# RWKV-7 scan with a hardswish FFN on one Trainium2 core: the PSUM layout and the order of the FFN after the first group

## The chip, the cores and the metric

The kernel runs on one core of one Trainium2 chip. The metric is the device time of one launch in microseconds; lower is better. Before the change the median of three runs is 794.57 us (792.73 to 795.51).

## The reference

Inputs are r, k, v, w, a, b of shape (batch 4, heads 8, time 768, head size 40) and two FFN matrices of 320 x 2048 and 2048 x 320, all float32. For every batch and head a 40 x 40 state is carried over time, and then the heads are joined to 320 features per token and go through the FFN:

```python
for t in range(S):
    y[:, :, t] = einsum('bhd,bhde->bhe', rt, state)
    Sa = einsum('bhde,bhe->bhd', state, at)
    state = state * wt[:, :, None, :] - einsum('bhd,bhe->bhde', Sa, bt) + einsum('bhd,bhe->bhde', vt, kt)
x = y.transpose(0, 2, 1, 3).reshape(B * S, H * D)   # 3072 x 320
h = x @ w_in
out = (h * clip(h + 3.0, 0.0, 6.0) / 6.0) @ w_out
```

## The kernel before, in words

**Units.** Time is cut into blocks of 64 steps. A unit is one such block for two batches, so its 128 tokens fill the 128 partitions. There are 24 units (`NK`), in groups of four (`NU`): 12 blocks of time by two pairs of batches. Neighbouring units belong to different pairs of batches, so a state is handed on from unit i to unit i + 2.

**Stages.** A unit is first prepared (`prepare`) and later stepped (`step`). Each stage is a generator: up to `yield PE` it issues its TensorE work into PSUM, after it the evictions by ScalarE (ACT) or VectorE (DVE). Preparing has W (turn w, copy it to `wm`, scan it to `prods`), gam (a second scan and the decay factors), A, B, K (turn and scale), F, factor, E and EV. Stepping has RT and VT (turn r and v), R, C, S (turn the state), U, UT, rS, H, y (output and new state) and the moves that bring the output to the FFN's layout. "Turn" is a transpose on TensorE against an identity matrix. `turn_pairs` (line 474) does it with four transposes of 128 x 128 into one bank. `turn_halves` (line 484) does it with eight of 64 rows each, even and odd ones into the two banks of a pair. In this kernel r and v are turned as halves from unit 4 on, a and b from unit 8 on; w and k are always turned as pairs, and the state in the same full-height form at line 879.

**Inversion.** Each group of four units needs the inverse of a triangular matrix. It is solved by `invert`, a side stream of about 67 small steps: 30 times a product (line 746) and a sum (line 752) on DVE, with three DVE transposes. `aside(n)` puts n of these steps into the instruction order. `third_block` finishes the inverse on TensorE (lines 781 and 804) into `tinv`.

**FFN.** A unit's FFN is two jobs, r = 0 and 1, each over half of the 2048 hidden columns. `expand` (line 1079) multiplies by w_in into two one-bank tiles `h`, in four pieces of four 128 x 128 matmuls, and then `short` adds the last 64 features (16 matmuls of 64 rows in the records). `results` makes `gt` out of each bank: a ReLU on ACT (line 1094), then a minimum and a product on DVE (line 1095), which reads the bank again. `contract` (line 1120) multiplies `gt` by w_out in four pieces of two matmuls 320 wide. The order of one stream is: expand of a job, then contract of the job before it. From unit 2 on both jobs of a unit add up in the one bank `o`, and ACT writes it out once as `ob` (line 1138); for units 0 and 1 each job is evicted by itself, as `part` by ACT (line 1130) and `ob` by DVE with `part` added (line 1135).

**Order.** The order on each engine is written out by hand. After the first group the loop goes over units 4 to 23 and in each over four blocks, 80 in all, numbered m. `a_block(m)` collects the stages that are due, those of stepping and those of preparing ahead. Where a unit ahead began at a multiple of four they are one part, otherwise two, and `together` issues a part: all TensorE products first, then all evictions in the order of `RESULTS`. `feed` puts FFN pieces between, by rates of 2.8, 3.5, 4.5 or 6.2 pieces per block (times 8/9 once `spread` is set), and 2 or 3 inversion steps per piece while an inversion is on. With `spread`, `short` of an open job is called in `together`, after the turns of W, S and K.

**PSUM.** It has eight banks. After the first group's FFN has begun they are: two pairs (four banks) for the stages, the bank `one` for the turns of W, S and K, the bank `o` for the FFN's output, and two banks `h`.

Of the kernel before, what the change touches and what calls it, by code (L numbers as in the profile page):

```python
# [16 lines left out]
P = 128  # L17
BL = 64
# [13 lines left out]
def kernel(  # L32
# [62 lines left out]
    ctx.enter_context(tc.manual_schedule())  # L95

    def bank(tag, shape, bufs):
        return ps.tile(shape, F32, name=tag, tag=tag, bufs=bufs)

    ring, open_half = deque(), [None]  # L100
    lent = tc.tile_pool(name="lent", bufs=1, space=PSUM)
    pools = {"lent": lent.__enter__(), "pair": ps}
    pairs = deque([("pair", 2), ("pair", 2), ("lent", 1)])

    def pair():
# [5 lines left out]
    def begun_ffn():  # L111

        lent.__exit__(None, None, None)
        pairs.clear()
        pairs.append(("pair", 2))
        pools["h"] = ctx.enter_context(tc.tile_pool(name="hidden", bufs=1, space=PSUM))

# [20 lines left out]

    shared = [None, 0]

    def ps_pair(*dims):

        n = 1
        for d in dims:
            n *= d
        if shared[0] is None or shared[1] + n > 512:
            shared[:] = pair(), 0
            open_half[0] = None
        at = shared[1]
        shared[1] += n  # L150
        views, step = [], n
        for d in dims:
            step //= d
            views.append([step, d])
        t = shared[0][:]
        return [_ap(t, at, views), _ap(t, at + 512, views), _ap(t, at, [[512, 2]] + views)]
# [56 lines left out]
    for t in wms:  # L213
        nc.vector.memset(t[:], 0.0)
    store = const.tile([P, 2 * H * BOTH], F32, name="store")
    slots = [store[:, n * H * BL:(n + 1) * H * BL].rearrange("p (h t) -> p h t", h=H) for n in range(3)]
    by_v, by_u = (store[:, n * H * BOTH:(n + 1) * H * BOTH].rearrange("p (h t) -> p h t", h=H) for n in range(2))
    inputs, others = {}, {}
# [310 lines left out]
    def prepare(i, F):  # L529
        n, o = i % NU, data[i]  # L530
        halves = i >= 2 * NU
        def w_stage():
            wt = turn_pairs(o["WN"])
            yield PE

            wm = o["wm"] = wms[i % 2]
            wv = wm[:, 0:SCAN].rearrange("p (r m i) -> p r m i", m=2, i=HB + 1)
            x = wt[:].rearrange("p r (q m i) -> p (r q) m i", q=2, m=2)
            if i == 0:
                nc.vector.tensor_copy(wv[:, :, 0, 1:HB + 1], x[:, :, 0, ::-1])  # L540
            else:
                nc.scalar.activation(out=wv[:, :, 0, 1:HB + 1], in_=x[:, :, 0, ::-1], func=AF.Copy)
            if i == 0:
                nc.vector.tensor_copy(wv[:, :, 1, 1:HB + 1], x[:, :, 1, :])
            else:
                nc.scalar.activation(out=wv[:, :, 1, 1:HB + 1], in_=x[:, :, 1, :], func=AF.Copy)  # L546
            fetch("W", following(i))
            prods = o["prods"] = tmp.tile([P, NB, 2, HB + 1], F32, name="prods", bufs=2)
            nc.vector.tensor_tensor_scan(  # L549
                out=prods[:].rearrange("p r m i -> p (r m i)"), data0=wm[:, 0:SCAN], data1=start[:],  # L550
                initial=0.0, op0=ALU.mult, op1=ALU.add,
            )
# [124 lines left out]
        def k_stage():  # L677
            x = turn_pairs(o["KN"])
            yield PE
            kt = o["kt"] = turned("kt")  # L680
            nc.vector.tensor_tensor(out=kt[:], in0=x[:], in1=o["rg"][:], op=ALU.mult)

# [142 lines left out]
    def step(i):  # L825
# [48 lines left out]
        def s_S():  # L874

            sp = ps_any([P, 2, 2, P])
            for q in range(2):
                for j in range(2):
                    nc.tensor.transpose(out=sp[:, q, j, :],
                                        in_=st[:, q, 2 * j:2 * j + 2, :].rearrange("p r d -> p (r d)"),  # L880
                                        identity=ident[:])
            yield PE
            S = m["S"] = grp.tile([P, 2, 2, P], F32, name="S", tag="S", bufs=1)
            nc.scalar.activation(out=S[:], in_=sp[:], func=AF.Copy)

# [157 lines left out]
    sums = {}  # L1043
    narrow, spread, LATEST = [], [False], 2

# [6 lines left out]
    def feed_forward():  # L1052

        last = None
        while True:
            while not available():
                if last:
                    yield from contract(*last)
                    last = None
                yield None  # L1060
# [12 lines left out]
    def expand(xt, j0, gts):  # L1073
# [17 lines left out]
        def results():  # L1091
            for c in range(2):
                gt = ffn.tile([P, NQ, P], F32, name="gt", bufs=5)
                nc.scalar.activation(out=gt[:], in_=hp[c][:], func=AF.Relu, bias=three[:], scale=1.0)  # L1094
                nc.vector.scalar_tensor_tensor(out=gt[:], in0=gt[:], scalar=6.0, in1=hp[c][:],  # L1095
                                               op0=ALU.min, op1=ALU.mult)
                gts.append(gt)

        narrow.append(short)
        for c in range(2):  # L1100
            for t in range(2):
# [3 lines left out]
                if c == 1 and t == 1 and not narrow:  # L1105
                    results()
                yield True
        if not spread[0] and narrow:
# [3 lines left out]
    def contract(i, r, gts):  # L1112
        split = i < SPLIT
        if r == 0 or split:
            op = bank("o", [P, 512], 1)[:, 0:DM]
        else:
            op = sums.pop(i)
        for c in range(2):
            for n in range(NQ):
# [4 lines left out]
                if n % 2 and (c == 0 or n < NQ - 1):  # L1124
                    yield True
        if r == 0:
# [5 lines left out]
        else:  # L1132
# [8 lines left out]
            for q in range(2):  # L1141
                row = (2 * p + q) * T + g * BL
                queue = nc.scalar if q and i == NK - 1 else nc.sync
                queue.dma_start(out=out[row:row + BL, :], in_=ob[half(q)])
        yield True

# [88 lines left out]
    for n, x in enumerate(BESIDE):  # L1235
# [6 lines left out]
        run(chains[int(x[0])], 1, MIXED if n >= 12 else 0)  # L1242
    TURNS_IN = [("one", 1), ("pair", 2), ("pair", 2)]
    blocks = {}
# [85 lines left out]
    for _ in range(18):  # L1330
# [12 lines left out]

    PRODUCTS = ["W", "S", "K", "RT", "VT", "A", "B", "factor",
                "y", "EV", "R", "C", "U", "UT", "rS", "H", "E", "F"]
    RESULTS = ["RT", "y", "W", "VT", "EV", "R", "S", "C", "A", "B", "move", "move2",
               "U", "UT", "rS", "F", "K", "H", "E", "factor", "beside", "gam"]
    TURNS = PRODUCTS[:3]
    WIDTH = {"R": NPR * D, "U": NPR * D, "y": NPR * BOTH, "EV": NPR * D}
    BLOCKS = 4  # L1350
    FIRST_NARROW = PRODUCTS[len(TURNS)]

    def together(stages):

        begun, banks = [], 0

        def finish():
            begun.sort(key=lambda x: RESULTS.index(x[0]))
            for _, rest in begun:
                for _ in rest:  # L1360
                    pass
            begun.clear()
            shared[0] = open_half[0] = None
            ring.clear()
            ring.extend(TURNS_IN)

        for name in PRODUCTS:
            if name == FIRST_NARROW and narrow and spread[0] and stages:
                narrow[0]()
            for stage in stages.get(name, []):  # L1370
                if name in TURNS:
                    need = 2 * (open_half[0] is None) if ring[0][0] == "pair" else 1
                else:
                    width = WIDTH.get(name, NPR * BL)
                    need = 2 * (shared[0] is None or shared[1] + width > 512)
                if banks + need > 5:
                    finish()
                    banks, need = 0, 1 if name in TURNS else 2
                banks += need
                rest = stage()  # L1380
                next(rest)
                begun.append((name, rest))
        begun.extend((name, stage()) for name in stages if name not in PRODUCTS
                     for stage in stages[name])
        finish()

# [24 lines left out]

    def feed(n, inversion):

        whole = int(n)
        for k in range(whole):
            pieces(1)
            aside(inversion)
        pieces(n - whole)

    for t in (by_v, by_u):  # L1420
        nc.gpsimd.memset(t[:, :, 0:BL], 0.0)
    del score[1:]
    m = 0
    for i in range(NU, NK):
        spread[0] = i >= 2 * NU - 1
        for j in range(BLOCKS):
            rate, inversion = 3.5, 0
            if i + AHEAD >= NK + NU - 1:
                rate = 4.5
            if i < 2 * NU - 1:  # L1430
                rate = 2.8
            parts = a_block(m)
            next(parts)
            if side or i % NU == NU - 1 and rate < 4:

                rate, inversion = 6.2, 2 + (i < 2 * NU)
            feed(rate / 2, inversion)
            for _ in parts:
                pass
            if i % NU < 2 and j < 2:  # L1440
                if i % NU == 0:
                    aside(3 * L)
                block(i, j)
            if side:
                rate, inversion = 6.2, 2 + (i < 2 * NU)
            feed(rate / 2, inversion)
            m += 1
# [37 lines left out]
```

## Time and profile before

| | |
|---|---|
| median of three runs | 794.57 us |
| time of the profiled execution | 794.59 us |
| its span, first to last instruction | 792.9 us |
| TensorE (PE) busy | 727.6 us, 92% of the span |
| PE busy with the FFN, lines 1079 and 1120 | 251.2 and 230.2 us |
| DVE, ACT, POOL busy | 496.8, 307.1, 161.5 us |
| mean granted TensorE clock | 0.961 of full speed |

The span is some 1.7 us shorter than the time of its execution, and the execution is that of the median to 0.02 us, so differences in the span can be set against the median. The first 196 us are the loading of the weights, the first group and the preparing of the second; the loop that the change rewrites starts near 196.6 us, and its last product of a step is followed by FFN work alone up to the end. The slices of the page are 19.8 us each.

### The profile page before, as it was taken

The numbers are of one execution on the slowest core, as the hardware profiler recorded it, in microseconds if no ns is written. First come the engines' busy times: TensorE is split into PE (matmuls) and PEld (weight loads), VectorE is DVE, ScalarE is ACT, GpSimd is POOL, SyncE is SP. The second block draws the span as 40 slices with busy tenths as digits, with TensorE's granted clock in tenths as the row PEclk, the third lists the DMA queues.
The fourth block names the chain that finished last, engine by engine and source line by source line (L and its number), as shares of the span: only waits on it lengthen the run. The fifth ranks groups of instructions, "written<-read, shape, count | busy, mean of one in ns | idle before, by whom it ended". The sixth has DMA issues, their size and how long they took to land.

```text
span 792.9 us, 32747 instructions
## 1 busy us (share of the span) xinstructions
PE 727.6 (92%) x14552; PEld 615.8 (78%) x14552; DVE 496.8 (63%) x986; ACT 307.1 (39%) x648; POOL 161.5 (20%) x296
## 2 busy tenths in 40 slices
PE   5735778999999999999999999999999999999997
PEld 4624667878778878888888888788888888888886
DVE  7898887689446699445898345888335982323210
ACT  2347663222553424443324453334443324412211
POOL 6403012421223203112303121303111201000000
PEclk9756898999999999999999999999999999999999
DMA  9683662420334321333323233223233101110100
GB/s 121 118 201 84 156 149 51 77 49 9 65 61 76 70 55 31 65 59 62 58 42 58 49 60 70 43 46 56 51 59 58 21 19 38 38 34 13 21 19 17
DMA packets 195004, 48.14 MB, mean 61 GB/s; under 512 B 178224, under 2 KB 193584, under 8 KB 194864
## 3 DMA queue, kind: packets, MB, share of 16 engines
q1 hardware_dynamic: 190560, 45.31, 30.9%
q8 instruction: 115, 1.88, 1.0%
q10 hardware_dynamic: 4304, 0.74, 0.7%
q14 instruction: 25, 0.20, 0.1%
HBM read 34.08 MB, written 3.93 MB: 48 GB/s over the span
## 4 chain that ended last, share of the span: by engine, by line
PE 76%; DVE 10%; issue 4%; DMA 3%; SPq 2%; ACT 2%; POOL 1%; DVEq 0%; POOLq 0%; ACTq 0%
PE h L1079 26%; PE o L1120 24%; PE pair L512 4%; PE pair L975 4%; PE one L474 2%; PE pair L484 2%; PE pair L893 2%; PE pair L861 2%; PE pair L695 1%; DVE wm L560 1%; DVE prods L549 1%; PE pair L929 1%; PE pair L913 1%; DVE prod L746 1%; DVE x L752 1%
## 5 line engine op out<-in xcount | busy, mean ns | idle before, releaser
L1079 PE MATMUL h<-xt,win 128*128 128x128 f32 (+1 forms) x2304 | 251.2, 283 | 4.9 <-DVE gt L1095 4.9
L1079 PEld LDWEIGHTS h<-xt,win 128*128 128x128 f32 (+1 forms) x2304 | 231.6, 193 | 23.0 <-issue 4.4
L1120 PE MATMUL o<-wout,gt 128*128 128x320 f32 x768 | 230.2, 443 | 0.0
L1120 PEld LDWEIGHTS o<-wout,gt 128*128 128x128 f32 x768 | 138.3, 190 | 50.7
L1094 ACT ACTIVATE gt<-h,three 128x512 f32<-128x512 f32 x96 | 63.1, 687 | 110.9 <-PE h L1079 110.5
L1095 DVE SCALAR_TENSOR_TENSOR gt<-gt,h 128x512 f32<-128x512 f32 x96 | 62.2, 683 | 67.2 <-ACT gt L1094 66.9
L746 DVE TENSOR_TENSOR prod<-x 128x30 f32<-128x30 f32 (+9 forms) x180 | 65.0, 361 | 9.0 <-POOL x L731 3.5
L525 DVE COPY_PREDICATED store<-mask,pair 128x512 f32<-128x512 int32 x40 | 29.0, 725 | 62.6 <-PE pair L512 62.5
L752 DVE TENSOR_TENSOR x<-x,prod 128x30 f32<-128x30 f32 (+9 forms) x180 | 64.4, 358 | 5.5
L668 POOL TENSOR_TENSOR KBt<-K,rgt 128x320 f32<-128x320 f32 x19 | 16.4, 865 | 204.5 <-ACT rgt L657 184.4
L983 POOL TENSOR_TENSOR yg<-ys,gam 128x512 f32<-128x512 f32 x20 | 25.5, 1273 | 147.5 <-DMA R<-in_r_dram 69.6
L982 DVE TENSOR_TENSOR ys<-pair,ys 128x512 f32<-128x512 f32 x20 | 13.8, 690 | 48.7 <-PE pair L975 43.5
L549 DVE TENSOR_TENSOR_SCAN prods<-wm,start 128x528 f32<-128x528 f32 x24 | 33.5, 1401 | 10.7 <-ACT wm L546 10.2
L839 ACT ACTIVATE RT<-pair 128x512 f32<-128x512 f32 x21 | 12.5, 597 | 59.1 <-PE pair L484 59.0
L975 PE MATMUL pair<-store,KBt 64*64 64x104 f32 x1280 | 33.1, 252 | 0.0
L560 DVE TENSOR_TENSOR_SCAN wm<-wm,start 128x528 f32<-128x528 f32 x24 | 31.1, 1297 | 0.8
L700 ACT ACTIVATE EV<-pair 64x320 f32<-64x320 f32 x44 | 18.9, 430 | 31.8 <-PE pair L695 30.4
L1138 ACT ACTIVATE ob<-o 128x320 f32<-128x320 f32 x22 | 9.6, 436 | 55.3 <-PE o L1120 34.6
L975 PEld LDWEIGHTS pair<-store,KBt 64*64 64x64 f32 x1280 | 29.1, 133 | 1.5
L814 ACT ACTIVATE tinv<-pair 32x256 f32<-32x256 f32 x48 | 18.0, 375 | 31.0 <-PE pair L804 30.4
L865 DVE TENSOR_TENSOR RR<-pair,EV 128x320 f32<-128x320 f32 x21 | 10.3, 489 | 23.7 <-PE pair L512 20.5
L897 ACT ACTIVATE store<-pair 128x320 f32<-128x320 f32 x24 | 10.5, 437 | 37.0 <-PE pair L913 33.6
(278 smaller groups left out, 1072.4 us busy)
## 6 DMA issues: line engine op xcount, KB each, us to landing
V<-in_v_dram SPq DMA_DIRECT2D x96, 40.0 KB
out_dram<-ob SPq DMA_DIRECT2D x47, 80.0 KB
R<-in_r_dram SPq DMA_DIRECT2D x92, 40.0 KB
B<-in_b_dram SPq DMA_DIRECT2D x42, 80.0 KB
store<-V SPq DMA_DIRECT2D x20, 160.0 KB
W<-in_w_dram SPq DMA_DIRECT2D x37, 80.0 KB
A<-in_a_dram SPq DMA_DIRECT2D x37, 80.0 KB
K<-in_k_dram SPq DMA_DIRECT2D x37, 80.0 KB
```

The costliest lines, as they stand in the source:

```text
L512: nc.tensor.matmul(out=o[i][half(q), n, :], lhsT=lhs[half(i, D), n ^ (2 * q * swap), half(q)], rhs=rhs[half(i, D), n ^ (2 * q * back), hal ...
L525: nc.vector.copy_predicated(out=x[:, :, 0:BL].rearrange("p (h i) t -> p i h t", i=2), mask=mask8, data=o[2])
L549: nc.vector.tensor_tensor_scan(out=prods[:].rearrange("p r m i -> p (r m i)"), data0=wm[:, 0:SCAN], data1=start[:], initial=0.0, op0=ALU.m ...
L560: nc.vector.tensor_tensor_scan(out=back, data0=back, data1=start[:], initial=0.0, op0=ALU.mult, op1=ALU.add)
L746: nc.vector.tensor_tensor(out=pv, in0=_ap(x[:], (i + 1) * L + i, [[L, n], [0, i]]), in1=_ap(x[:], i * L, [[0, n], [1, i]]), op=ALU.mult,)
L752: nc.vector.tensor_tensor(out=rest, in0=rest, in1=pv, op=ALU.add)
L975: nc.tensor.matmul(out=y[q][half(s), pr, :], lhsT=o[name][half(q), h * D:h * D + SLOT], rhs=m[name][half(q), x, :], start=(name == "K" and ...
L983: nc.gpsimd.tensor_tensor(out=yg[:], in0=m["ys"][:].rearrange("p r q t -> p r (q t)"), in1=o["G"][:], op=ALU.mult)
L1079: nc.tensor.matmul(out=hp[c][:, i, :], lhsT=lhsT, rhs=rhs, start=(begun[c] == 0), stop=(begun[c] == 3 * NQ - 1))
L1094: nc.scalar.activation(out=gt[:], in_=hp[c][:], func=AF.Relu, bias=three[:], scale=1.0)
L1095: nc.vector.scalar_tensor_tensor(out=gt[:], in0=gt[:], scalar=6.0, in1=hp[c][:], op0=ALU.min, op1=ALU.mult)
L1120: nc.tensor.matmul(out=op[:], lhsT=gts[c][:, n, :], rhs=wout[:, c * HJ + r * NQ + n, :], start=((split or r == 0) and c == 0 and n == 0), ...
```

## The change

The first group, up to the loop, keeps its order but for the size of a ring of buffers (`gt`, four in place of five) and the place of three buffers in SBUF. From the loop on:

- The FFN is first led to a fixed place (`held`): the job in hand is expanded and the one before it is contracted. Then the banks `one`, `o` and the two `h` are given back. Two of them become a third pair, the other two are `h` again.
- `contract` has no bank of its own. It takes the next of the two `h` buffers, which is the bank of the first product of the job that was just expanded. So both jobs of a unit are evicted one by one: `part` by ACT for the first, `ob` by DVE for the second.
- w and k (from unit 8 on) and the state (from unit 4 on) are turned as halves, in pairs of banks.
- `together` deals a part's products to three pairs (`dealt`), mixing as few pairs as possible between those that ACT and those that DVE evicts. `short` comes ahead of all products of a block.
- Both parts of a block are issued one after the other, and the FFN pieces come after them, a number per block from the table `GAPS`. A feed also ends where a job has been expanded. `third_block` goes into the middle of a feed. Inversion steps go by the table `SHARES`: so many after each kind of piece (2, 0, 1, 0 after the four of expand, 3, 3, 3, 2 after the four of contract), one more per piece before unit 8, one within `results` and one per `together`.

```diff
-        return ps.tile(shape, F32, name=tag, tag=tag, bufs=bufs)
+        return singles.tile(shape, F32, name=tag, tag=tag, bufs=bufs)
...
         def w_stage():
-            wt = turn_pairs(o["WN"])
+            wt = turn_halves(o["WN"])[2] if halves else turn_pairs(o["WN"])
...
         def k_stage():
-            x = turn_pairs(o["KN"])
+            x = turn_in(o["KN"], halves)
...
         def s_S():
-            sp = ps_any([P, 2, 2, P])
+            sp = ps_pair(4, SLOT) if halves else ps_any([P, 2, 2, P])
...
+                    if halves:
+                        for s in range(2):
+                            nc.tensor.transpose(out=sp[s][:, 2 * q + j, :], in_=x[half(s)],
+                                                identity=ident[half(s), half(s)])
...
+    SHARES = "20103332111"
+    held, dense = [False], [False]
...
         def results():
             for c in range(2):
-                gt = ffn.tile([P, NQ, P], F32, name="gt", bufs=5)
+                gt = ffn.tile([P, NQ, P], F32, name="gt", bufs=4)
                 nc.scalar.activation(out=gt[:], in_=hp[c][:], func=AF.Relu, bias=three[:], scale=1.0)
+                if c == 0 and dense[0]:
+                    aside(int(SHARES[9]))
...
     def contract(i, r, gts):
-        split = i < SPLIT
-        if r == 0 or split:
+        split = i < SPLIT or dense[0]
+        if dense[0] and spread[0]:
+            op = pools["h"].tile([P, 512], F32, name="h", tag="h", bufs=2)[:, 0:DM]
+        elif dense[0]:
+            op = pair()[:, 0, 0:DM]
+        elif r == 0 or split:
             op = bank("o", [P, 512], 1)[:, 0:DM]
...
+        if todo and narrow and spread[0]:
+            narrow[0]()
+        while todo or others:
+            n = len(todo)
+            while dealt([x[0] for x in todo[:n]]) is None:
+                n -= 1
+            groups = dealt([x[0] for x in todo[:n]])
...
+            begun.sort(key=lambda x: RESULTS.index(x[0]))
+            aside(int(SHARES[10]))
...
+    def feed(n, more, beside=None):
+        for k in range(n):
+            if beside and k == n // 2:
+                beside()
+                beside = None
+            said = next(stream)
+            if said is None:
+                break
+            aside(int(SHARES[said - 1]) + more)
+            if said == ENDED:
+                break
...
+    held[0] = True
+    while next(stream):
+        pass
+    held[0] = False
+    ended = hidden.pop()
+    ended.__exit__(None, None, None)
+    single.__exit__(None, None, None)
+    pools["third"] = ctx.enter_context(tc.tile_pool(name="third", bufs=1, space=PSUM))
+    pools["h"] = ctx.enter_context(tc.tile_pool(name="later", bufs=1, space=PSUM))
+    pairs.append(("third", 1))
+    pairs.appendleft(("pair", 2))
+    dense[0] = spread[0] = True
...
+    GAPS = "22231244621448824244222244844844242444244484884461144244448448482142442664444423"
     for i in range(NU, NK):
-        spread[0] = i >= 2 * NU - 1
         for j in range(BLOCKS):
-            rate, inversion = 3.5, 0
...
-            parts = a_block(m)
-            next(parts)
-            if side or i % NU == NU - 1 and rate < 4:
-                rate, inversion = 6.2, 2 + (i < 2 * NU)
-            feed(rate / 2, inversion)
-            for _ in parts:
+            n = int(GAPS[m])
+            for _ in a_block(m):
                 pass
+            beside = None
             if i % NU < 2 and j < 2:
                 if i % NU == 0:
                     aside(3 * L)
-                block(i, j)
-            if side:
-                rate, inversion = 6.2, 2 + (i < 2 * NU)
-            feed(rate / 2, inversion)
+                beside = lambda: block(i, j)
+            feed(n, int(SHARES[8]) * (i < 2 * NU), beside)
             m += 1
```

## The prediction

> **What bounds the kernel now.** I read the page first, then the busy time of each engine in stretches of 20 us, then the waits from 200 us on, the chain that ended last between 300 and 420 us, and the timeline where one FFN job passes over to the next.
>
> ```profile
> PE 727.6 (92%) x14552; PEld 615.8 (78%) x14552; DVE 496.8 (63%) x986; ACT 307.1 (39%) x648; POOL 161.5 (20%) x296
> ...
> PE   5735778999999999999999999999999999999997
> ...
> DVE  7898887689446699445898345888335982323210
> ```
>
> PE is at 9 tenths or more in every slice after the first eight, and all that the change touches (from 196.6 us on) lies there. DVE reaches 8 and 9 tenths in the slices with an inversion only. The stretches give it in numbers (PE, PEld, DVE, ACT and POOL busy, then granted clock, DMA share and GB/s):
>
> ```profile
> 280.00:300.00 20.00, 18.99 (x356) 16.77 (x357) 18.83 (x49) 6.97 (x15) 0.00 (x0) 1.00 0.24 47
> ...
> 440.00:460.00 20.00, 20.00 (x428) 17.08 (x424) 8.24 (x14) 10.13 (x24) 5.35 (x9) 1.00 0.36 62
> ```
>
> The first is a stretch with an inversion, the second one without. Adding up 20 minus PE busy over the 29 stretches from 200 to 780 us gives 7.7 us of idle PE, nearly all of it in stretches with an inversion; the clock is 1.00 in all of them. So filling PE better can bring 7.7 us at most, and anything beyond that must be work taken from PE. Who PE waits for, from the list of waits (total, times, longest):
>
> ```profile
> PE h L1079 <- DVE gt L1095: 2.8, 3, 1.0
> ```
>
> **Part 1: w, k and the state as halves.** The chain shows PE work end to end, so a row's length there is what the work takes of PE:
>
> ```profile
> 355.85 0.95 PE pair L512 x64
> 356.81 1.27 PE o L1120 x4
> 358.08 1.78 PE h L1079 x16
> 359.87 0.44 PE one L474 x4
> 360.30 1.09 PE h L1079 x16
> 361.39 0.49 PE pair L484 x16
> 361.88 1.59 PE pair L975 x64
> 363.47 1.98 PE h L1079 x16
> 365.45 1.08 PE o L1120 x4
> 366.53 0.44 PE one L879 x4
> ```
>
> A turn as a pair (four transposes, line 474, and line 879 for the state) takes 0.44 us. Two turns as halves (16 transposes, line 484) take 0.49 us, so one takes 0.245. The change replaces w and k in units 8 to 23 (16 each) and the state in units 4 to 23 (20), 52 turns: 52 x (0.44 - 0.245) = 10.1 us less on PE. A second way: the rows of line 474 are busy 9.7 us for 16 turns (0.61 each), those of line 484 for a and b 7.1 and 6.6 us for 16 (0.43): 52 x 0.18 = 9.4. I take 10.1 with bounds of 9 and 11. This is in a stretch where PE is the bound and lies on the path. The evictions keep their shapes (128 x 512, or 128 x 256 twice for w) and their engines, so they cost nothing more.
>
> What speaks against it is a change of the array's form. The row for that: the first piece after products of 40 or 64 rows takes 1.27 or 1.98 us, while the next ones take 1.08 and 1.78, so entering full-height work costs 0.2 us. The turned halves stand among others of 64 rows, so I add no such entry. [...]
>
> **Part 2: the FFN's output in the bank of its first product.** No PE work is added. It takes away the bank `o`, and it adds a wait: the first matmul of `contract` must wait until DVE has made `gt` from the first bank. Behind it on PE stands everything, since PE works in order. The timeline shows the length of that path where the ReLU follows `short` at once:
>
> ```profile
> 380.45 1.16 PE L1079 MATMUL h<-xt,win 64*128 64x128 f32 x16
> ...
> 381.64 1.27 ACT L1094 ACTIVATE gt<-h,three 128x512 f32<-128x512 f32 x2 [2.00 <-PE h L1079]
> ...
> 382.63 1.28 DVE L1095 SCALAR_TENSOR_TENSOR gt<-gt,h 128x512 f32<-128x512 f32 x2
> ...
> 383.34 1.88 PE L1120 MATMUL o<-wout,gt 128*128 128x320 f32 x6
> ```
>
> `short` ends at 381.61. The first of the two DVE instructions ends at 382.63 + 0.64 = 383.27, 1.66 us later, and the block's products kept PE busy until 383.34, when `contract` begins. So the new wait would just have been covered. At four other such places (ends of `short` at 216.82, 246.58, 417.14 and 497.99) the path took 1.40, 1.40, 1.39 and 1.65 us. After the change `short` stands ahead of a block's products. They take about 1.8 us (E, EV, H and factor, as here: 0.24 + 0.60 + 0.95), 2.1 (A, B, R, C, S: 0.49 + 0.60 + 0.49 + 0.245 and the rest of the state's halves), 2.3 (K, U, UT, rS, F) or 2.6 us (RT, VT, W, y with 1.59). Cover is there in each, by 0.1 to 0.9 us, so long as DVE is not behind.
>
> Where is it behind? The block with y, W and gam leaves DVE about 5.1 us: y 0.69 + 0.39 + 0.49 and the two scans 1.47 + 1.31 with 0.25 + 0.28 + 0.34 around the second. By the table, the pieces of six such blocks are one expand (m = 12, 28, 36, 44, 52, 60), 3.6 us, then `short` 1.1 and ReLU 0.7. So DVE comes free about when it is needed, and 0.7 us or so late where two to four inversion steps (0.36 each) come in: some 4 x 0.7 = 2.8 us. Of the three waits of `h` on `gt` (2.8 us in all) I take most as gone, since `results` no longer stands behind a block's scans, and the two halves of part 2 as +0.5 together. Bounds: -2.8 (only those waits go) and +16 (0.4 us at each of the 41 contractions).
>
> The eviction changes sides: 21 `ob` go from ACT (0.437) to DVE (0.484, line 1135) and 21 `part` on ACT (0.438, line 1130) come in their place. ACT stays as it is, DVE gets 21 x 0.484 = 10.2 us more. Outside of inversions DVE is busy 8 to 13 of 20 us and it costs nothing. Inside, some two per inversion fall in stretches where it is at 18.8 of 20: at worst 4 x 2 x 0.48 = 3.9 us, at best nothing; I take 1.
>
> **Part 3: both parts of a block back to back, three pairs.** From m = 16 on a block has one part (units ahead begin at multiples of four), and its products fitted the five banks before, as they fit three pairs now: RT and VT, y, W; or A and B, R and C, S; or K, U and UT, rS and F. So the third pair buys room for the halves and no more. From m = 3 to 14 there are two parts, which before had half a feed between them. In seven of these blocks (m = 5, 6, 8, 9, 11, 12, 14) the two need four or five pairs, so PE waits at the fourth for an eviction of 0.6 to 0.7 us with its start and end: up to 1 us each, +7 at worst. On the other side twelve entries into full-height work are saved (12 x 0.2 = 2.4). I take +2, bounds -2.4 and +7.
>
> **Part 4: the table.** I counted the stream by it: a job's eight pieces go on as before, 297 pieces fall into the 80 blocks and three jobs with the rest of a fourth are left for the end, where PE has the FFN alone, as it has now in its last 50 us. Pieces moved from one place to another where PE is busy cost nothing; both kernels have the same number. Five blocks get one piece (1.1 us) only (m = 4, 10, 49, 50, 65), where the evictions that the next block needs take some 2 us after the last product while its own first products can begin: +1, bounds 0 and +5. Of the other idle time (7.7 - 2.8 = 4.9 us) I take 2 as gone, bounds 4.9 and none. The drain ahead of the loop moves some four pieces forward into a stretch (180 to 200 us) that has no idle PE: nothing, at worst +1.5 for banks that are still being read.
>
> **The sum**, from the profiled execution of 794.6 us (that of the median): -10.1 + 0.5 + 1 + 2 + 1 - 2 = -7.6 with the clock as it was, so 787.0 us.
>
> **Rivals.** *The output waits for DVE* (slower). In ten of the 24 jobs that I followed, DVE took up `gt` 4.0 to 7.2 us after the ReLU began, in place of 0.7 to 1.0, since scans and evictions of a block stood ahead of it (for example ReLU at 392.06, `gt` at 397.56). Now PE would stand still for that. Five such places at some 4 us are 20 us: 794.6 - 10.1 + 20 = 804. It decides from 10.1 / 41 = 0.25 us of mean wait per contraction on. Against it: `results` now comes ahead of a block's evictions, not behind them. 0.14.
> *The crowding eats the gain* (no change): part 3 at +7, the one-piece blocks at +4, none of the old idle time gone: 794.6 - 10.1 + 11 = 795.5. For it speaks that PE has almost no idle time now, so any new wait is visible. 0.09.
> *Halves are no cheaper there* (slower): eight transposes in place of four with one entry each (+0.2 as above): 797. Against it are the 16 in 0.49 us. 0.05.
> The forecast has 0.72; its own range is 780 to 792, from all waits at their low ends (-10.1 - 4.9) and from part 2 and part 3 at +5 beyond what I took.
>
> **Chances and range.** A measurement of this kernel can tell about 0.3% (2.4 us) from no change. The forecast falls into faster, the crowding mostly into no change and a little into faster, the other two into slower: faster 0.74, same 0.08, slower 0.18. For 8 in 10 the range takes the forecast and the near ends of the rivals: 778 to 798.
>
> **What would show it.** The transposes of w, k and the state as rows of 64 rows, eight per turn, and PE busy lower by about 10 us over the span. The waits should list `o` (now in `h`) waiting for `gt` with a few us in all; over 10 us there means the first rival, and then the stretches with DVE above 18 of 20 should be those where PE falls. Idle PE between 200 and 300 us would be the crowding. I am wrong in kind if the clock in the loop falls below 1.00, or if the matmuls of the FFN themselves change in spacing.

## The result and the profile after

The changed kernel takes 805.9 us (median of 4 runs, 803.54 to 807.91) against 795.04 us of the kernel before in 4 runs: a ratio of 1.0141, interval 1.0101 to 1.0181. It is slower by about 11 us, where 787.0 us was forecast. The profiled execution took 804.31 us, its span is 802.3 us, 9.4 us longer than that of before.

The page after, its first rows:

```profile
PE 725.6 (90%) x14760; PEld 612.4 (76%) x14760; DVE 503.2 (63%) x1007; ACT 307.8 (38%) x648; POOL 160.6 (20%) x296
...
PE   5735669999999889999999899999999999999998
...
DVE  7898797688553599455697355698356774323211
...
PEclk9756798999999989999999999999999999999999
```

PE is busy 2.0 us less than before, not 10, and it now dips in the fourteenth, fifteenth and twenty-third slices (261 to 301 and 441 to 461 us). The granted clock has a dip in the fifteenth slice (near 290 us), where before it had none past the seventh. The stretches of 20 us give it in numbers (length, then PE, PEld, DVE, ACT, POOL busy, granted clock, DMA share, GB/s):

```profile
280.00:300.00 20.00, 16.55 (x202) 13.65 (x203) 19.04 (x47) 3.99 (x9) 4.02 (x9) 0.83 0.35 60
300.00:320.00 20.00, 19.43 (x357) 16.40 (x357) 18.34 (x42) 9.14 (x18) 2.50 (x3) 1.00 0.10 20
...
400.00:420.00 20.00, 18.24 (x259) 15.03 (x258) 19.07 (x44) 3.95 (x8) 3.98 (x8) 0.91 0.39 69
...
440.00:460.00 20.00, 17.84 (x460) 15.00 (x462) 8.21 (x16) 9.76 (x24) 4.37 (x6) 0.91 0.31 54
...
520.00:540.00 20.00, 18.09 (x270) 15.38 (x269) 19.07 (x44) 3.94 (x8) 3.93 (x8) 1.00 0.36 65
```

Two losses are to be read here. From 200 to 780 us PE stands idle 18.8 us (20 minus PE busy, added up) where it was 7.7 us before. And the clock, which had been 1.00 in all of these stretches, falls: adding up length times (1 - clock) over stretches of 5 us gives 6.8 us of full-speed time.

For a ledger both kernels are cut at the same piece of work: the end of the last expand ahead of the loop, with the same 3048 matmul records before it. From there to the end, first before, then after:

```profile
196.52:792.90 596.38, 584.53 (x11506) 492.57 (x11504) 333.53 (x653) 226.99 (x496) 111.31 (x188) 1.00 0.26 47
```

```profile
197.04:802.30 605.26, 582.76 (x11714) 489.76 (x11712) 339.95 (x674) 227.59 (x496) 109.98 (x188) 0.99 0.26 46
```

This part is 8.9 us longer; the other 0.5 us of the 9.4 lie ahead of it. A run below has the same 11714 matmuls of the new order with the clock at 1.00 throughout, and there they keep PE busy for 577.0 us. So the ledger is: 7.6 us less PE work (584.53 to 576.97), 5.8 us of clock in busy PE (576.97 to 582.76; the rest of the 6.8 falls into idle time), and 10.7 us more idle PE (length minus busy: 22.50 against 11.85).

The waits of PE from 200 us on (total, times, longest):

```profile
PE h L1161 <- DVE gt L1132: 6.0, 6, 1.9
PE h L1114 <- DMA xt<-yg: 3.5, 2, 2.1
PE pair L646 <- issue: 2.8, 4, 1.5
PE pair L520 <- ACT RT L858: 1.5, 1, 1.5
PE pair L714 <- issue: 1.2, 1, 1.2
PE pair L880 <- DVE score L529: 0.9, 1, 0.9
```

Line 1161 is `contract`, now writing into `h`: its wait for `gt` is the one that the change added. The second row is an expand whose input had not landed. "issue" is time in which the profile shows nothing that PE waited for. How the first row comes about is in the chain of after, from 400 to 420 us:

```profile
405.18 0.60 DVE ys L1008
...
406.70 1.56 DVE prods L567
...
408.57 1.32 DVE wm L578
...
410.16 0.35 DVE rgam L591
410.51 0.32 DVE x L771
...
411.74 0.41 DVE prod L765
...
412.17 0.70 DVE gt L1132
412.87 0.04 issue
412.92 6.06 PE h L1161 x16
```

This is m = 28 and 29. The block with y, W and gam leaves DVE the output sum, two scans and the copies; then the order puts four inversion steps; only then comes `gt`. The ReLU had begun at 409.36, so `gt` came 2.8 us later, not 0.7. PE stood still for 1.8 us. And then eight matmuls 320 wide (16 records) took 6.06 us; at full clock the same work takes 4.57, as a row further down shows.

### The profile page after: what moved, and what is told of

The parts are those of the page before. It is cut to its first block, busy times and chain, and to the rows that moved or that the text cites. A ratio compares the mean times of both kernels' runs of the same rounds, so it can differ in the third digit from the quotient of the medians.

```text
span 802.3 us, 33218 instructions
## 1 busy us (share of the span) xinstructions
PE 725.6 (90%) x14760; PEld 612.4 (76%) x14760; DVE 503.2 (63%) x1007; ACT 307.8 (38%) x648; POOL 160.6 (20%) x296
## 4 chain that ended last, share of the span: by engine, by line
PE 69%; DVE 14%; SPq 6%; issue 4%; ACT 3%; DMA 3%; POOL 0%; DVEq 0%; POOLq 0%; ACTq 0%
PE h L1114 24%; PE h L1161 19%; PE o L1161 3%; PE pair L1001 3%; SPq L466 2%; PE pair L520 2%; SPq L463 2%; PE pair L492 2%; DVE prod L765 2%; DVE x L771 2%; PE pair L1161 2%; DVE gt L1132 2%; DVE prods L567 1%; PE third L1161 1%; PE pair L714 1%
## 5 line engine op out<-in xcount | busy, mean ns | idle before, releaser
L1161 PE MATMUL h<-wout,gt 128*128 128x320 f32 x592 | 179.4, 451 | 6.0 <-DVE gt L1132 6.0
L1161 PEld LDWEIGHTS h<-wout,gt 128*128 128x128 f32 x592 | 110.1, 194 | 50.1 <-DVE gt L1132 6.9
L533 DVE COPY_PREDICATED beside<-mask,pair 128x512 f32<-128x512 int32 x25 | 18.1, 725 | 44.4 <-PE pair L520 44.4
L1161 PE MATMUL o<-wout,gt 128*128 128x320 f32 x96 | 30.3, 458 | 0.0
L1171 ACT ACTIVATE part<-h 128x320 f32<-128x320 f32 x19 | 8.3, 437 | 50.8 <-PE h L1161 50.6
L719 ACT ACTIVATE EV<-pair 64x320 f32<-64x320 f32 x36 | 15.5, 430 | 28.5 <-PE pair L714 19.0
L1001 PE MATMUL pair<-beside,KBt 64*64 64x104 f32 x960 | 24.9, 252 | 0.6 <-PE pair L492 0.6
L596 POOL COPY rgam<-prods 128x256 f32<-128x256 f32 x22 | 24.5, 1112 | 0.0
L833 ACT ACTIVATE tinv<-pair 32x256 f32<-32x256 f32 x44 | 16.5, 375 | 19.7 <-PE pair L823 19.1
L1001 PEld LDWEIGHTS pair<-beside,KBt 64*64 64x64 f32 x960 | 21.9, 133 | 1.7 <-PE pair L492 0.7
L1176 DVE SCALAR_TENSOR_TENSOR ob<-h,part 128x320 f32<-128x320 f32 x18 | 8.8, 490 | 22.8 <-PE h L1161 21.7
L1161 PEld LDWEIGHTS o<-wout,gt 128*128 128x128 f32 x96 | 17.7, 195 | 6.7 <-issue 0.4
```

What stands on the lines that cost most here:

```text
L533: nc.vector.copy_predicated(out=x[:, :, 0:BL].rearrange("p (h i) t -> p i h t", i=2), mask=mask8, data=o[2])
L596: nc.gpsimd.tensor_copy(rv[:, :, 0:HB], o["prods"][:, :, 0, 0:HB][:, :, ::-1])
L1001: nc.tensor.matmul(out=y[q][half(s), pr, :], lhsT=o[name][half(q), h * D:h * D + SLOT], rhs=m[name][half(q), x, :], start=(name == "K" and ...
L1161: nc.tensor.matmul(out=op[:], lhsT=gts[c][:, n, :], rhs=wout[:, c * HJ + r * NQ + n, :], start=((split or r == 0) and c == 0 and n == 0), ...
```

## The experiments

Each kernel ran beside the kernel before on the same chip; the numbers in brackets are the ratio to it and its interval. Idle PE and clock loss are those from 200 to 780 us of each profile, as above.

**Inversion steps away from the end of expand.** Changed kernel, one table:

```diff
-    SHARES = "20103332111"
+    SHARES = "00004443101"
```

> The changed kernel with another table of inversion steps: none after the pieces of expand and none within results (2, 0, 1 and 1 before), in their place 4, 4, 4, 3 after the pieces of contract (3, 3, 3, 2 before); the same 15 steps per job. Theory (the output's new wait, lengthened by inversion steps that the order puts between the end of expand and the first gt, and a clock that falls in the pause): the wait of h for gt falls from 6.0 us in all to about 1.5, the granted clock stays at 1.00 near 290 and 412 us, and the time falls by 4 to 5 us of waits and some 4 us of clock, to 796 to 799. Rival (DVE has no room in the inversions, so steps moved only move the wait): idle PE between 200 and 660 us stays at 18 us or so and the time at 804 to 807.

Measured: 803.29 us (1.0128, 1.0104 to 1.0152), 4 us above the theory's range and just under the rival's; idle 19.9 us, clock loss 6.8 us. `contract` waits for `gt` 5.0 us in place of 6.0, and the two longest, of 2.1 us, are where they were (m = 29 and 45). A new wait of 2.1 us for `kt` came at m = 14. The steps moved into `contract` ran on into the block with y, so DVE began y later. This speaks for the rival: moving steps by the kind of piece moves the wait.

**Expands a block later, where their input was late.** Changed kernel, three digits of `GAPS` (m = 10 from 1 to 0, m = 33 from 4 to 2, m = 34 from 2 to 4):

```diff
-    GAPS = "22231244621448824244222244844844242444244484884461144244448448482142442664444423"
+    GAPS = "22231244620448824244222244844844224444244484884461144244448448482142442664444423"
```

> The changed kernel with four entries of the table of pieces changed: m = 10 from 1 to 0 and m = 11 from 4 to 4 as it is (now a whole expand), m = 33 from 4 to 2 and m = 34 from 2 to 4, so that a job's expand starts a block later after the move of its unit's output. Theory (two expands start before their input has landed, 3.5 us of waiting for xt, and the pause near 448 us takes the clock down): both waits go, the clock stays at 1.00 near 450 us, 800 to 803. Rival (the pieces are then missing elsewhere and another wait takes their place): 804 to 807 with idle PE as before.

Measured: 800.46 us (1.0090, 1.0072 to 1.0108). Waits for `xt` are gone, idle is 15.4 us in place of 18.8 and the clock no longer falls near 450 us. Against the changed kernel that is some 4 us by the ratios (5.4 by the medians, which come from two sets of runs), within the range that the theory gave. 3.3 us of it are seen as less idle PE. A gain of clock is not seen: the loss is 6.8 us as it was, since the pause for `gt` near 525 us, after which the clock had stayed at 1.00 in the changed kernel, took it down in this profile. The three pauses for `gt` stay (6.9 us of such waits in all).

**Both.** The two edits above together.

> Both edits together. If waits and clock are the cause and independent: 791 to 795, so about the time of the kernel before. If DVE is the limit in the inversions: 802 to 806.

Measured: 800.51 us (1.0089, 1.0072 to 1.0106), no better than the second alone and outside both ranges; idle 16.5 us, waits for `gt` 4.8 us. As in the first, a new wait for `kt` came, of 2.3 us.

**The turns at full height again.** Changed kernel, w, k and the state turned by four transposes each, into one bank of a pair of their own:

```diff
-            wt = turn_halves(o["WN"])[2] if halves else turn_pairs(o["WN"])
+            wt = turn_wide(o["WN"]) if halves else turn_pairs(o["WN"])
...
-    WIDTH = {"R": NPR * D, ...
+    WIDTH = {"W": 512, "K": 512, "S": 512, "R": NPR * D, ...
```

> The changed kernel with w, k and the state turned at full height again, each into one bank of a pair that it has to itself; the products still fit three pairs per block, and tables and order are unchanged. Theory (a turn as halves is cheaper by 0.15 to 0.2 us of PE, 52 turns): slower than the changed kernel by 7 to 10 us, 812 to 816, PE busy 732 or more. Rival (in this order each turn as halves pays an entry and gains nothing): 804 to 807.

Measured: 814.74 us (1.0262, 1.0234 to 1.0289), 8.8 us above the changed kernel; its page:

```profile
PE 738.2 (91%) x14552; PEld 622.0 (77%) x14552; DVE 503.6 (62%) x1007; ACT 306.2 (38%) x648; POOL 160.9 (20%) x296
```

From the end of the last expand ahead of the loop PE is busy 592.4 us here, 9.6 us more than in the changed kernel, although the clock lost less (3.4 us). So the halves do save about what was worked out, in this very order, and the loss lies elsewhere.

**No expand right after the block with y.** The second experiment's table with m = 12 to 16 as 2, 2, 8, 8, 6 and m = 27 to 31 (43 to 47, 59 to 63) as 8, 2, 2, 4, 8 in place of 4, 4, 8, 4, 4.

> The changed kernel with the table of pieces set so that no expand ends right after a block that leaves y and two scans to DVE while an inversion is on (m = 12, 28, 44, 60), beside the entries of e2_gaps: m = 12 to 16 get 2, 2, 8, 8, 6; m = 27 to 31, 43 to 47 and 59 to 63 get 8, 2, 2, 4, 8. The same pieces in all. Theory (the three pauses of some 2 us come from DVE's y and scans standing ahead of gt, and each takes the clock down): h waits for gt for under 2 us in all, the clock stays at 1.00 through the loop, 787 to 792. Rival (DVE is short of room while an inversion is on, so the pause comes elsewhere): 798 to 802 as with e2_gaps.

Measured: 814.73 us (1.0248, 1.0223 to 1.0273), far off. Idle 24.0 us, clock loss 13.7 us. PE's longest waits:

```profile
PE pair L919 <- DVE bt L619: 8.0, 2, 4.0
PE pair L880 <- DVE score L529: 3.5, 1, 3.5
...
PE h L1161 <- DVE gt L1132: 2.1, 3, 1.5
```

Most of the waits for `gt` did go (2.1 us are left), but the blocks with y and the one after it now had two pieces each, and DVE, with steps in those pieces too, fell 4 us behind at `bt`. The same DVE work stood in the way at another place, and the clock fell after it. So the pauses depend on the amount of DVE work in those blocks, against PE work to cover it, and not on the output's bank alone.

**Two parts of a block with pieces between them.** The same, with half of a block's pieces back between its parts for m = 5, 6, 8, 9, 12 and 14:

```diff
+            parts = a_block(m)
+            next(parts)
+            if m in (5, 6, 8, 9, 12, 14):
+                feed(n // 2, ...)
```

> e4_order with half of a block's pieces put back between the two parts in m = 5, 6, 8, 9, 12 and 14. Theory (parts back to back cost PE a few us of waiting for evictions before m = 16, between 205 and 290 us): idle PE there falls by 2 to 4 us, and the time by as much against e4_order. Rival (the waits there are for the DMA of PE's own instructions and do not depend on the order): no difference, within 1 us.

Measured: 815.26 us (1.0258, 1.0238 to 1.0278), no difference from the one above. Idle PE fell by 1.3 us and the clock's loss grew by 1.6. In this order the parts back to back are not where the time went; it is the rival's outcome, though not its reason, which this run does not show.

**The pause filled with work.** The second experiment with four matmuls of 128 x 256 whose output nobody uses, at the end of the products of m = 13, 29 and 45:

```diff
+            if now[0] in (13, 29, 45):
+                for c in range(4):
+                    nc.tensor.matmul(out=spare[0][0][:, c % 2, 256:512], lhsT=win[:, 0, 0:P],
+                                     rhs=win[:, 0, 0:256], start=True, stop=True)
```

> e2_gaps with four extra matmuls of 128 x 256 (some 1.7 us of PE, their output is not used) at the end of the products of m = 13, 29 and 45, where PE would stand still for gt. No wait is taken away. Theory (about half of what the pauses cost is the clock that falls after them): the clock stays at 1.00 near 290, 410 and 530 us and the time falls by 4 to 6 us against e2_gaps, to 794 to 797. Rival (the clock falls for another reason, or its fall costs nothing since DVE sets the pace there): 799 to 803.

Measured: 803.9 us (1.0102, 1.0073 to 1.0131), so the expected gain of the whole did not come. But the two places near 410 and 530 us show what was asked. The timeline of PE at m = 29, first without, then with the extra work (line 1435):

```profile
404.97 0.67 PE L520 MATMUL third<-RT,VT 40*64 40x64 f32 x32
407.56 6.26 PE L1161 MATMUL h<-wout,gt 128*128 128x320 f32 x16 [1.91 <-DVE gt L1132]
413.66 4.83 PE L1114 MATMUL h<-xt,win 128*128 128x128 f32 x48
```

```profile
413.95 0.67 PE L520 MATMUL third<-RT,VT 40*64 40x64 f32 x32
414.55 1.99 PE L1435 MATMUL pair<-win 128*128 128x256 f32 x8
416.39 4.57 PE L1161 MATMUL h<-wout,gt 128*128 128x320 f32 x16
```

`contract` begins about as late, 2.6 and 2.4 us after the start of the last products, but takes 4.57 us and not 6.26. The time from unit to unit there (between their turns of r) falls from 35.5 to 33.7 us at 410 and from 35.5 to 33.8 at 530: 1.7 us, with PE busier than before. In the changed kernel the stretch at 530 us has a pause of 1.9 us with the clock staying at 1.00, and it too takes 33.8 us, so the 1.7 us are the clock's. The pause of 1.9 us thus cost nearly as much again, 1.7 us, by the clock that fell after it. At m = 13 the extra work did harm (43.4 to 45.9 us and 28.5 to 31.4 in the next unit): a wait of 3.4 us for `kt` grew there, and the clock fell after that one.

**The third pair's banks to the output.** Changed kernel, two banks of the output's own, products dealt to two pairs:

```diff
-    pools["third"] = ctx.enter_context(tc.tile_pool(name="third", bufs=1, space=PSUM))
+    pools["o"] = ctx.enter_context(tc.tile_pool(name="own", bufs=1, space=PSUM))
...
-            op = pools["h"].tile([P, 512], F32, name="h", tag="h", bufs=2)[:, 0:DM]
+            op = pools["o"].tile([P, 512], F32, name="o", tag="o", bufs=2)[:, 0:DM]
```

> The changed kernel with the two banks of the third pair given to the FFN's output instead (two of its own), and the products of a block dealt to two pairs; halves, table and order unchanged. Theory (the output's wait for gt is 6 us with 5 us of clock behind it, but the halves need the third pair): the waits of the output for gt go, while blocks of three groups are issued in two steps with a wait for evictions between them, some 0.7 to 1 us in each of about 55 blocks; 830 to 860. Rival (the third pair is not needed, its banks serve the output better): 794 to 798.

Measured: 852.37 us (1.0716, 1.0692 to 1.0741), idle 51.4 us, clock loss 18.9 us:

```profile
PE pair L520 <- ACT S L908: 23.5, 13, 4.0
PE pair L1001 <- ACT RT L858: 9.2, 11, 2.8
PE pair L646 <- DVE kt L700: 7.9, 10, 1.7
```

The time is in the expected range, and the waits for `gt` are no longer among the longest: in this order the halves need the third pair. That w, k and the state now take half a pair each, where they had a bank of their own, is the likely reason.

**Inversion steps told off by block.** The second experiment's order, with no steps in m = 12, 28, 44, 60 and fewer around them, more in the blocks that leave DVE little to do (the lines of the table `STEPS` are shortened):

```diff
-            aside(int(SHARES[said - 1]) + more)
+            aside(int(STEPS[m][k]) if m in STEPS else int(SHARES[said - 1]) + more)
+    STEPS: m = 26 "44433010", 27 "2222", 28 "0000", 29 "33322010", 30 "4442", 31 "2121", ...
```

> e2_gaps with the same order of pieces, but inversion steps told off by block where an inversion is on: none at all in and right after the blocks with y and scans that end with an expand (m = 12, 28, 44, 60), more in the blocks that leave DVE little (m = 26, 30, 31 and those like them: 19, 14 and 6 in place of 14, 11 and 3). Theory (gt comes late because DVE still has steps, y and scans ahead of it, and without the steps the scans end just about when gt is needed): the waits for gt fall from 6.9 us to under 2, the clock stays at 1.00 near 290, 410 and 530 us, 788 to 793. Rival (DVE has no room in an inversion, whatever the placing): the waits come elsewhere, 798 to 803.

Measured: 794.18 us (1.0011, 0.9992 to 1.0029; 12 runs), 6.3 us below the second experiment and level with the kernel before, just above the range that the theory gave and well below the rival's. Waits for `gt` are 2.8 us in place of 6.9, none longer than 0.7; the clock loss is 3.4 us and lies at 230 and 440 us, after pauses of another kind.

**The inversions' products and sums left out**, 30 of each per inversion past the first group (lines 746 and 752 of the kernel before), in the kernel before and in the second experiment; their outputs lack that part:

```diff
+            if alone:
                 nc.vector.tensor_tensor(out=pv, ..., op=ALU.mult)
...
+            if alone:
                 nc.vector.tensor_tensor(out=rest, in0=rest, in1=pv, op=ALU.add)
```

> The kernel before without the 30 products and 30 sums of the inversions past the first group (lines 746 and 752; the order and all else stay, the rest of an inversion too). It says what DVE's part in the inversions costs this order. If PE is the bound there anyway: 789 to 793 (the waits for DVE, some 4 us, gone, and some 1 us before the loop).

> e2_gaps without the same 30 products and sums. Theory (the saving of the halves is there, and only DVE's load in the inversions, with the clock that falls in the pauses, takes it back): 783 to 787, faster than n_before by 4 to 8 us. Rival (the new order loses on PE itself, by waits for evictions and instructions): 792 to 798, no faster than n_before.

Measured: 788.42 us (0.9935, 0.9917 to 0.9954) for the kernel before, just under the expected range, and 786.59 us (0.9914, 0.9894 to 0.9934) for the other. Their pages, the kernel before first:

```profile
PE 727.8 (92%) x14552; PEld 617.4 (78%) x14552; DVE 394.4 (50%) x686; ACT 307.5 (39%) x648; POOL 162.0 (21%) x296
```

```profile
PE 717.3 (92%) x14760; PEld 606.9 (78%) x14760; DVE 401.7 (51%) x707; ACT 308.0 (39%) x648; POOL 159.5 (20%) x296
```

DVE's steps cost the old order 793.9 - 788.4 = 5.5 us and the new one 800.5 - 786.6 = 13.9 us. In both profiles here the clock is 1.00 through the loop, so PE busy can be set side by side there. From the end of the last expand ahead of the loop, the kernel before first:

```profile
195.28:788.50 593.22, 584.11 (x11506) 492.41 (x11504) 250.97 (x412) 226.01 (x494) 109.03 (x182) 1.00 0.25 47
```

```profile
192.79:782.70 589.91, 576.97 (x11714) 485.42 (x11712) 259.03 (x433) 226.40 (x494) 106.35 (x182) 1.00 0.26 48
```

PE has 7.1 us less to do and stands idle 3.8 us more (12.9 against 9.1), so the new order is 3.3 us shorter. The pages' totals would say more than that, 10.5 us less PE busy and a span 5.8 us shorter, but 3.4 and 2.5 us of these lie ahead of the loop, where both do the same matmuls and the clock happened to cost 27.3 us in place of 30.7. The medians differ by 1.8 us, less than the 4 to 8 expected, and the intervals overlap: that the new order is faster without the steps is not clear of the noise. Of the idle time, 3.7 us in three pauses within the products of F (line 646) and 1.2 us at line 714 are marked "issue".

**Fewer steps still.** The one told off by block, with none of the single steps in m = 27, 43, 59, none after the last three pieces of the block ahead of them, and more in m = 31, 47, 63:

> e8_steps with no inversion steps in the blocks m = 27, 43 and 59 beside those of their feed, and the last three pieces of the feed before without any, since the output still waited 0.7 us there in each inversion; the steps go to m = 31, 47 and 63. Theory (each such wait is what DVE has ahead of gt): the three waits of 0.7 us go, 791 to 793, at or just under the kernel before. Rival (what is left is the waits for PE's own instructions and the clock, which the steps don't touch): 793 to 796.

Measured: 798.05 us (1.0040, 1.0014 to 1.0066). The three waits of 0.7 us fell to 0.3, but `contract` at m = 32, 48 and 64 now waits 1.54, 1.54 and 1.27 us, as the inversion's last steps fell into the block with y. In the first of these places it is ACT that is late: it copies both halves of the inverse into `tinv` (2.1 us, line 786) before the ReLU, where the run above has a ReLU between the two. Neither outcome came: the time is above both ranges. No complete version here is clearly faster than the kernel before.

## Why the prediction was wrong

The forecast was 7.6 us less than before, the profile has 9.4 us more. Of these 17 us, 8.2 are idle PE (taken as +2.5 in all, measured +10.7), 5.8 are clock (taken as nothing), 2.5 are PE work (taken as -10.1, measured -7.6), and 0.5 lie ahead of the loop.

**Part 1 was right on the turns, too high for the whole.** 10.1 us was worked out from 0.44 and 0.245 us per turn, with 9 as the lower bound. PE's work in the loop fell by 7.1 us in the pair without the inversions' products, and by 7.6 against the kernel before. Undoing the halves cost 8.8 us of time and 9.6 us of PE busy, so the turns are worth about what was worked out, and the rest of the change added PE work that the sum had not counted. Which part of it did is not shown. In the timeline of after, one turn follows the other by 0.25 to 0.34 us:

```profile
276.65 0.46 PE L492 MATMUL pair<-ident,R 64*128 64x64 f32 x8 [0.20 <-ACT F L656]
276.95 0.41 PE L492 MATMUL third<-ident,V 64*128 64x64 f32 x8
277.20 0.41 PE L492 MATMUL third<-ident,W 64*128 64x64 f32 x8
```

At 0.25 to 0.34 us per turn, where 0.245 was counted, there is no room for an entry of 0.2 us each. The third rival put one on each of the 52 turns (52 x 0.2 = 10.4 us, 787.0 + 10.4 = 797.4); no run shows such an entry for a turn as halves, and these rows, which stand among other work of 64 rows, show none.

**Part 2 failed, in the step that put the lateness of `gt` at 0.7 us in four places.** The place was the right one (the block with y and two scans, an expand, then the output): after three of the six blocks named (m = 12, 28 and 44) PE waited, but 1.8 to 1.9 us each. The working counted 5.1 us of DVE from the end of the products; the trace has DVE still busy with earlier steps when those products end, and four more steps between the scans and `gt`. The net +0.5 us should have been +3.2 (6.0 of waits less the 2.8 that went). The first rival had the mechanism, with too high a price for a single place. That its 804 us lie near the measured 805.9 is luck: they came from 20 us of such waits, and 6.0 were measured.

**A term was missing: the clock.** The text said that a clock below 1.00 would prove it wrong in kind, and gave it no price and no reason why a new pause should leave it alone. It cost 6.8 us in the profiled execution, 5.8 of them in busy PE, and nothing between 200 and 780 us in that of before.

**Part 4 failed, in the step "pieces moved from one place to another where PE is busy cost nothing".** The table starts two expands before their input has landed: 3.5 us of waiting, and a fall of the clock worth 1.7 us after one of them. Neither is in the second experiment, which is some 4 us shorter.

**Part 3** was counted at +2. Idle PE between 200 and 300 us did grow, from 3.4 to 8.5 us (one wait of 1.5 us for RT's eviction at m = 12 is of the kind described), but putting pieces between the parts again did not shorten the time in the one order where it was tried. That the third pair is needed for the halves was right.

**The "issue" pauses** were not foreseen: 4 us in after (lines 646 and 714), 1.1 us of this kind in before. The longest recur at the same places in most profiles of the new order: 1.2 us ahead of the first product of line 714 at m = 8, 1.1 to 1.8 us in the middle of the products of line 646 at m = 18, and 1.3 to 1.9 us there at m = 34 in the profiles where it comes. What they wait for was not tested and stays open.

So the gain was made and spent: 7.6 us of PE work against 10.7 us more idle PE and 5.8 us of clock. The shown causes are DVE's steps (8.4 us more in the new order than in the old by the medians, 8.6 in the loops of the profiles) and the two early expands (some 4 us by the ratios, 3.6 in the loops). With the expands later and the steps left out of both orders, the new loop is 3.3 us shorter than the old one: 3.6 + 8.6 - 3.3 is the loop's 8.9 us. With the steps told off by block and the expands later, the kernel is level with the one before; what keeps it from the other 7 us is only argued: the pauses marked "issue", small waits for DVE, and the clock after them.

## What to carry to other kernels

A saving on a full engine is worth what the order leaves of it: ask what each engine has queued ahead of a new wait, from the end of the block before and not from the moment the wait begins, with every small step that a side stream puts there. Where PE had run without a gap, a new pause of 1.9 us cost 3.6 us where the clock fell after it (the second experiment near 410 us), and 1.9 where it did not (the changed kernel near 531 us). And a table of how much work goes where has to be checked against the landing of inputs and against the load of the second engine, block by block.

## What the runs showed of the hardware

In the loop of after the granted clock of TensorE falls to 0.50 three times, in pauses of PE of 1.8, 1.8 and 2.1 us (before the products at 290.90, 412.92 and 450.19 us), and is back at 1.00 after 6.8, 3.4 and 3.4 us. The first of these by stretches:

```profile
286.00:289.00 3.00, 2.06 (x94) 1.88 (x90) 2.77 (x11) 1.75 (x3) 0.85 (x3) 1.00 0.56 95
289.00:291.00 2.00, 0.19 (x9) 0.10 (x1) 1.90 (x6) 0.00 (x0) 0.00 (x0) 0.67 0.32 64
291.00:296.00 5.00, 5.00 (x10) 3.23 (x11) 4.83 (x13) 0.00 (x0) 0.00 (x0) 0.50 0.12 32
```

It does not fall each time: after the pause of 1.9 us at 531 us it stayed at 1.00, in the same execution. In the run with fewer steps still, the clock lost 1.7 us each near 250, 300 and 335 us, where PE had paused for 1.25, 0.93 and 1.50 us, and stayed at 1.00 around pauses of 1.54 us at 433 and 549 us.

The falls keep to a grid in both profiled executions. In after, those of the loop begin at 289.67, 412.55 and 450.10 us, and the distances, 122.88 and 37.55 us, are 36 and 11 times 3.413. All ten falls of that execution and all nine of that of before lie whole multiples of 3.413 us apart within their profile. Carried on, by an estimate from these numbers, the grid has a line at 532.0 us. It divides the pause of 1.9 us (531.34 to 533.25), so that only 0.7 us lay ahead of it; at 411 us, where the clock fell, 1.4 of 1.8 us did. Whether that is why the clock stayed at 1.00 is not shown.

Where a fall of 3.4 us to 0.50 comes alone, the loss is half of that: 1.7 us at 450 us in after, and 1.7 us each near 410 and 530 us in the second experiment.
